# Strassen operand sums and bias additions on VectorE alone, and `state@w_in` casts on ScalarE, in an attention-to-MoE kernel

## Chip, cores and metric

The kernel runs on one core of a Trainium2 chip. The metric is the device time in microseconds (us); 241.25 us is the median of three runs before the change. Engines are called by their short names: PE (TensorE), PEld (its weight loads), DVE (VectorE), ACT (ScalarE), POOL (GpSimd), SP (SyncE, here a DMA queue).

## What is computed

A cross attention between tokens and a small state, in both directions, and then a dense feed-forward block with a squared ReLU. There are 8 batches (B) of 8 heads, 512 tokens (S), 32 state rows (Ns) and a head size of 64; d_model is 512, d_ff 2048.

```python
def _attn_ref(x, state):
    B, H, S, D = x.shape
    scale = 1.0 / np.sqrt(D)
    a = softmax(scale * np.matmul(x, state.transpose(0, 1, 3, 2)))
    xread = np.matmul(a, state)                      # S rows a batch
    a2 = softmax(scale * np.matmul(state, x.transpose(0, 1, 3, 2)))
    sread = np.matmul(a2, x)                         # Ns rows a batch
    return np.concatenate([xread, sread], axis=2)

def _moe_ref(x, w_in, w_out, s, b):
    r = np.maximum(x @ w_in, 0.0)
    g = s * (r * r) + b
    return g @ w_out
```

(`softmax` stands for the written-out subtraction of the maximum, exponential and division.) The inputs are float32; the kernel computes with float16 operands and float32 accumulation.

## The kernel before

**Stages.** The token rows of one batch are one stage `s`. Since `xread @ w_in` is `a @ (state @ w_in)`, the kernel first makes `M` = state@w_in for a batch (`att_M`, four column blocks `c` of 512, evacuated from PSUM as fp16), and the normalised attention weights `a4` (`att_T`, `att_D`: scores, exponential `E`, sum, logarithm `L`, reciprocal `R`, product). Then `mm1_x(s, f)` multiplies the two into `h` for each of 16 blocks `f` of d_ff (two matmuls of 128x512). ACT takes the ReLU `r` of each `h` (line 321), DVE squares two of them at a time into `g` (line 327, 128x1024). The stage of batch `s` also does, in pieces between its 16 steps f, the attention and the `M` of batch `s+1` (`pieces`), and the second matmul of batch `s-1`.

**The second matmul.** For batches 1 to 6 (`fast`) the product `g @ w_out` is done with seven block products p1 to p7 in place of eight (a Strassen level, Winograd's form). It needs operand sums: four of weights, `wd0` to `wd3`, each in two halves `j`, made once (`weight_sums`, on POOL, during stage 1 from f=8 on), and four of tokens for each batch, `s1` to `s4`, each in two halves `j` (`token_sum`; `s1`, `s2` and `s4` on DVE, `s3` on POOL). All are 128x1024 in fp16.

**Products and banks.** `fast_items` gives the matmuls in the order p1, first half of p6, first half of p2, second half of p6, second half of p2, p7, p5, p4, p3. p1 and p2 accumulate in one PSUM bank (`oA`), p6, p7 and p4 in a second (`oB`), p5 and p3 in a third tile (`oC`), out of two buffers. Partial sums are read out on the way, in `done`: after p1, ACT copies the bank scaled to `q`, and POOL makes `qa` and `qb` from it, with the two halves of the bias added; after p6, DVE makes `u2` from the bank and `qa`, and p7 may only then accumulate onto it; after p7, `u3`. `put` makes the output `osb` on DVE and issues its DMA on POOL's queue. p6 needs `s2` and `wd1`, p7 `s3` and `wd2`, p5 `s1` and `wd0`, p4 `wd3`, p3 `s4`. The first 16 products of batch `s` run in the last three steps of stage `s`, the others in stage `s+1`.

**What sets the order.** PE, SP and POOL run in the order in which the code is written (`manual_schedule`); DVE and ACT are ordered by a scheduler when the program is built, and then run in that order, one instruction after another. Semaphores make an instruction wait for its operands and for its buffer. Batch 0, batch 7 and the state rows go without the Strassen level; `late` holds their evacuations until the bias is there (`bias_end`, at f=4 of stage 1). The line number 66 stands for all matmuls.

Of the kernel before, what the change touches and what calls it, by code (L numbers as in the profile page):

```python
# [14 lines left out]
def kernel(  # L15
# [298 lines left out]
    def mm1_close(key, hps, ntok, f):  # L314
        if f % 2 == 0:
            R2[key] = rpool.tile([P, 2, ntok], FP16, name=f"r_{key}_{f}", tag="r")
        r16 = R2[key]
        if key == 0 and f in (1, 5):
            nc.vector.tensor_scalar(r16[:, f % 2], hps, 0.0, None, ALU.max)
        else:  # L320
            nc.scalar.activation(r16[:, f % 2], hps, AF.Relu)  # L321
        if f % 4 == 0:
            G4[key, f // 4] = gpool.tile([P, 4, ntok], FP16, name=f"g_{key}_{f}", tag="g")
        gt = G4[key, f // 4]
        G[key, f] = gt[:, f % 4]
        if f % 2 == 1:
            nc.vector.tensor_mul(gt[:, f % 4 - 1 : f % 4 + 1], r16, r16)  # L327

    def mm1_k(b, f, g, hps):
        a = A[b]  # L330
# [66 lines left out]
                late.pop()()  # L397


    NH = DM // 2  # L400
    TH = S // 2

    def weight_sums():
        out = []
        for j in range(2):
            b11, b12 = wo[j][:, :, 0:NH], wo[j][:, :, NH:DM]
            b21, b22 = wo[2 + j][:, :, 0:NH], wo[2 + j][:, :, NH:DM]
            t1, t2, t3, t4 = (wd[i][j] for i in range(4))
            out += [(t1, b12, b11), (t2, b22, t1), (t3, b22, b12), (t4, b21, t2)]
        return [lambda o=o, a=a, c=c: nc.gpsimd.tensor_sub(o, a, c) for o, a, c in out]  # L410

    SQ = {}

    def token_sum(b, i, j):
        SQ[b, i, j] = spool.tile([P, 4, TH], FP16, name=f"s{i}_{b}_{j}", tag="s")
        o = SQ[b, i, j]
        a11, a21 = G4[b, j][:, :, 0:TH], G4[b, j][:, :, TH:S]
        if i == 3:
            nc.gpsimd.tensor_sub(o, a11, a21)  # L419
            return  # L420
        a12, a22 = G4[b, 2 + j][:, :, 0:TH], G4[b, 2 + j][:, :, TH:S]
        if i == 1:
            nc.vector.tensor_add(o, a21, a22)  # L423
        elif i == 2:
            nc.vector.tensor_sub(o, SQ[b, 1, j], a11)  # L425
        else:
            nc.vector.tensor_sub(o, a12, SQ[b, 2, j])  # L427

    def fast_items(b):
        acc = {}  # L430
        kept = {}

        def lhs(p, k, i):
            c = P * i
            if p == 1:
                return G[b, k][:, c : c + P]
            if p == 2:
                return G[b, 8 + k][:, c : c + P]
            if p == 4:
                return G[b, 8 + k][:, TH + c : TH + c + P]  # L440
            si = {3: 4, 5: 1, 6: 2, 7: 3}[p]
            return SQ[b, si, k // 4][:, k % 4, c : c + P]

        def rhs(p, k):
            if p == 1:
                return wof(k)[:, 0:NH]
            if p == 2:
                return wof(8 + k)[:, 0:NH]
            if p == 3:
                return wof(8 + k)[:, NH:DM]  # L450
            ti = {4: 3, 5: 0, 6: 1, 7: 2}[p]
            return wd[ti][k // 4][:, k % 4, :]

        def keep(name):
            kept[name] = upool.tile([P, 2, NH], FP32, name=f"{name}_{b}", tag=name)
            return kept[name]

        def put(bank, add, j, n0):
            osb = opool.tile([P, 2, NH], FP32, name=f"osb_{b}_{j}_{n0}", tag="osb")
            nc.vector.scalar_tensor_tensor(osb, acc[bank], s_bc, add, ALU.mult, ALU.add)  # L460
            dst = out_BSn[b, 0:S].rearrange("(q ci cj) n -> cj q ci n", ci=2, cj=2)
            nc.gpsimd.dma_start(dst[j][:, :, n0 : n0 + NH], osb)  # L462

        def blk(n0):
            return bias_bc[:, n0 : n0 + NH].unsqueeze(1).broadcast_to([P, 2, NH])

        def done(p):
            if p == 1:
                q = keep("q")
                nc.scalar.activation(q, acc["A"], AF.Copy, scale=s_bc)  # L470
                nc.gpsimd.tensor_add(keep("qa"), q, blk(NH))
                nc.gpsimd.tensor_add(keep("qb"), q, blk(0))
            elif p == 6:
                u = keep("u2")
                nc.vector.scalar_tensor_tensor(u, acc["B"], s_bc, kept["qa"], ALU.mult, ALU.add)  # L475
            elif p == 2:
                put("A", blk(0), 0, 0)
            elif p == 7:
                u = keep("u3")
                nc.vector.scalar_tensor_tensor(u, acc["B"], s_bc, kept["qa"], ALU.mult, ALU.add)  # L480
            elif p == 5:
                put("C", kept["u3"], 1, NH)
            elif p == 4:
                put("B", kept["qb"], 1, 0)
            else:
                put("C", kept["u2"], 0, NH)

        def item(p, k, i):
            bank = {1: "A", 2: "A", 6: "B", 7: "B", 4: "B", 5: "C", 3: "C"}[p]
            fresh = p in (1, 6, 5)  # L490
            if fresh and k == 0 and i == 0:
                acc[bank] = psO.tile([P, 2, NH], FP32, tag="o", name=f"o{bank}_{b}")
# [87 lines left out]
    with tc.manual_schedule(engines={ET.PE, ET.SP, ET.Pool}):  # L580
# [89 lines left out]
        def pieces(s):  # L670
# [3 lines left out]
            def at(f, fn):  # L674
                out.setdefault(f, []).append(fn)

            if s == 1:
                at(0, lambda: att_xT_dma(2))
                at(0, gated_x3)
                at(0, lambda: att_ET(0))  # L680
                at(0, lambda: att_ET(1))
                at(8, lambda: att_xT_dma(3))
                at(12, lambda: load_x(4))
                at(5, lambda: att_M(1, 3, "act"))
                at(2, bias_sum)
                at(3, lambda: att_M(1, 2, "dve"))
                at(4, bias_end)
                at(6, lambda: att_stT(2))
                at(7, lambda: att_M(2, 0, "dve"))
                at(8, lambda: att_M(2, 1, "act"))  # L690
                at(10, lambda: att_M(2, 2, "dve"))
                at(10, lambda: att_T(2, [0, 1]))
                at(11, lambda: att_ET(2))
                at(12, lambda: att_D(2, [0, 1]))
                at(13, lambda: att_M(2, 3, "act"))
                return out
            if s + 3 < B:
                at(13 if s == 2 else 9, lambda: load_x(s + 3))
            if nb < B:
                at(0, lambda: att_stT(nb))  # L700
                at(3, lambda: att_T(nb, [0, 1]))
                at(3, lambda: att_M(nb, 0, "dve"))
                at(4, lambda: att_ET(nb))
                if nb + 1 < B:
                    at(4, lambda: att_xT_dma(nb + 1))
                at(5, lambda: att_D(nb, [0, 1]))
                at(7, lambda: att_M(nb, 1, "dve"))
                at(7, lambda: att_M(nb, 2, "act"))
            at(10, lambda: att_V(s))
            at(11, lambda: att_srT(s))  # L710
            if nb < B:
# [14 lines left out]
        for s in range(1, B):  # L726
# [13 lines left out]
            for f in range(NKF):  # L740
# [1 line left out]
                    token_sum(s - 1, 4, 1)  # L742
                mm1_x(s, f)
                if s in fast:
                    if f in (3, 7):
                        token_sum(s, 3, f // 4)
                    if f in (11, 12, 13):
                        token_sum(s, (1, 2, 4)[f - 11], 0)
                    if f == 15:
# [1 line left out]
                        token_sum(s, 2, 1)  # L751
                for fn in todo_s.get(f, []):
                    fn()
                if s == 1 and f >= 8:
                    sums.pop(0)()
                for fn in items[f]:
                    fn()
                if s == last_b and f in (14, 15):
# [37 lines left out]
```

## Time and profile before

| what | us |
|---|---|
| median of 3 runs (241.06 to 241.54) | 241.25 |
| the profiled execution | 241.94 |
| its span, first to last instruction | 240.1 |
| PE busy | 211.6 |
| DVE busy | 168.9 |
| ACT busy | 124.7 |
| POOL busy | 103.5 |

The span runs from stage 0 (until about 30 us) over stage 1 (30 to 56) and stage 2 (to about 96) to the steady stages 3 to 6 (23.3 us each, to 189), stage 7 and the tail. In the rows, a tile is named without its number: `s` is one of `s1` to `s4`, told apart by the line (419 is `s3`, 423 `s1`, 425 `s2`, 427 `s4`), `wd` one of `wd0` to `wd3`, `u` at line 475 is `u2` and at 480 `u3`. What stands in brackets at the end of a row is the time for which the engine was idle just before, and who released it.

### The profile page before, as it was taken

The page shows a single profiled execution, that of the slowest core. Times are in us where ns is not written, and L with a number is a line of the kernel's source. Part 1 is how long each engine was busy: PE and PEld are TensorE (multiplying, and loading weights), DVE is VectorE, ACT ScalarE, POOL GpSimd, SP SyncE. Part 2 cuts the span into 40 slices and gives each one's busy share as a digit, 9 for nine tenths or more (in the row PEclk, how much of TensorE's full clock was granted, in tenths as well). Part 3 has the DMA queues.
Part 4 walks back from the last instruction along what each step waited for, and adds up shares of the span by engine and source line. Part 5 has one row for each costly group of instructions (what it writes and reads, how often), then busy time and mean ns, then how long its engine had stood idle before and what let it go on. Part 6 is the DMA issues. An engine that isn't in the chain of part 4 may idle for free.

```text
span 240.1 us, 4655 instructions
## 1 busy us (share of the span) xinstructions
PE 211.6 (88%) x1916; PEld 127.3 (53%) x1916; DVE 168.9 (70%) x241; ACT 124.7 (52%) x217; POOL 103.5 (43%) x104
## 2 busy tenths in 40 slices
PE   7887898894717999979998999899899999999993
PEld 3323333342403576656764676467557767766553
DVE  1696649589997569868896699669966995342321
ACT  3786534485103673667566756665576645433200
POOL 6930014699971342646164626342624440211033
PEclk9999999999575899999999999999999999999999
DMA  6999989951700119561919281811131201121223
GB/s 199 208 206 203 198 103 176 207 98 48 128 0 0 46 51 201 102 133 46 176 44 147 39 169 45 177 45 53 38 87 46 87 3 44 46 87 44 87 46 87
DMA packets 38776, 23.72 MB, mean 99 GB/s; under 512 B 24100, under 2 KB 36644, under 8 KB 38756
## 3 DMA queue, kind: packets, MB, share of 16 engines
q0 software_dynamic: 15792, 16.72, 35.2%
q1 hardware_dynamic: 22548, 6.62, 13.4%
q8 instruction: 15, 0.25, 0.4%
q10 hardware_dynamic: 416, 0.10, 0.2%
q14 instruction: 5, 0.04, 0.1%
HBM read 17.33 MB, written 8.91 MB: 109 GB/s over the span
## 4 chain that ended last, share of the span: by engine, by line
PE 56%; DVE 28%; DMA 7%; issue 4%; ACT 2%; POOL 1%; SPq 0%; DVEq 0%
PE h L66 14%; DVE g L327 10%; PE oB L66 10%; PE o L66 9%; PE oC L66 8%; DMA xn<-in_x_dram 5%; DVE s L425 4%; DVE s L427 4%; PE h_sr L66 3%; PE o_sr L66 3%; DVE s L423 3%; PE Mps L66 3%; PE oA L66 3%; DMA xf<-in_x_dram 2%; DVE u L475 2%
## 5 line engine op out<-in xcount | busy, mean ns | idle before, releaser
L321 ACT ACTIVATE r<-h 128x512 f16<-128x512 f32 x126 | 73.8, 596 | 80.2 <-PE h L66 73.4
L66 PE MATMUL h<-a,M 128*128 128x512 f16 x256 | 76.9, 387 | 6.4 <-DVE a L239 5.9
L327 DVE TENSOR_TENSOR g<-r 128x1024 f16<-128x1024 f16 x64 | 56.7, 893 | 21.3 <-ACT r L321 21.2
L66 PEld LDWEIGHTS <-g 128*128 128x128 f16 x432 | 41.4, 99 | 24.6 <-issue 5.6
L66 PEld LDWEIGHTS <-s 128*128 128x128 f16 x384 | 36.5, 100 | 29.9 <-issue 10.2
L419 POOL TENSOR_TENSOR s<-g 128x1024 f16<-128x1024 f16 x12 | 25.4, 2118 | 35.0 <-DVE g L327 34.9
L66 PE MATMUL oB<-wd,s 128*128 128x256 f16 x192 | 29.7, 285 | 11.8 <-DVE s L425 6.7
L462 POOL DMA_DIRECT2D out_dram<-osb x24 | 16.5, 686 | 51.3 <-DVE osb L460 42.5
L66 PEld LDWEIGHTS <-M 128*128 128x128 f16 x256 | 24.9, 99 | 16.3 <-DVE a L239 5.5
L66 PE MATMUL o<-wo,g 128*128 128x512 f16 (+1 forms) x144 | 32.3, 356 | 0.9 <-DVE osb L368 0.9
L66 PE MATMUL oA<-wo,g 128*128 128x256 f16 x192 | 28.6, 278 | 0.3 <-DVE osb L368 0.3
L265 DVE CAST M<-Mps 128x1024 f16<-128x1024 f32 x15 | 18.3, 1218 | 1.6 <-PE Mps L66 1.6
L425 DVE TENSOR_TENSOR s<-s,g 128x1024 f16<-128x1024 f16 x12 | 14.5, 1208 | 0.2
L66 PE MATMUL Mps<-wi,stT 64*32 64x512 f16 x256 | 12.7, 391 | 1.9 <-DVE stT L153 1.0
L66 PE MATMUL oC<-wd,s 128*128 128x256 f16 x96 | 14.3, 273 | 0.0
L66 PE MATMUL oB<-wd,g 128*128 128x256 f16 x96 | 13.6, 273 | 0.0
L263 ACT CAST M<-Mps 128x1024 f16<-128x1024 f32 x13 | 13.1, 1011 | 0.6
L66 PE MATMUL oC<-wo,s 128*128 128x256 f16 x96 | 13.4, 273 | 0.0
L427 DVE TENSOR_TENSOR s<-g,s 128x1024 f16<-128x1024 f16 x12 | 13.0, 1083 | 0.2
L66 PEld LDWEIGHTS <-stT 64*32 64x32 f16 x384 | 5.0, 91 | 14.0 <-issue 8.8
L321 ACT ACTIVATE r_sr<-h_sr 128x256 f16<-128x256 f32 x16 | 6.1, 382 | 10.7 <-PE h_sr L66 10.7
L460 DVE SCALAR_TENSOR_TENSOR osb<-oC,s_bc,u 128x512 f32<-128x512 f32 x12 | 9.0, 748 | 2.8 <-PE oC L66 2.8
(80 smaller groups left out, 231.5 us busy)
## 6 DMA issues: line engine op xcount, KB each, us to landing
out_dram<-osb POOLq DMA_DIRECT2D x31, 256.0 KB, 2.5
xn<-in_x_dram POOLq DMA_DIRECT2D x7, 512.0 KB, 6.3
wi<-in_moe_w_in_dram POOLq DMA_DIRECT2D x4, 512.0 KB, 8.7
wo<-in_moe_w_out_dram POOLq DMA_DIRECT2D x4, 512.0 KB, 16.2
xf<-in_x_dram SPq DMA_DIRECT2D x2, 512.0 KB, 4.8
out_dram<-osb_sr POOLq DMA_DIRECT2D x8, 64.0 KB, 2.0
out_dram<-osb SPq DMA_DIRECT2D x2, 128.0 KB
st<-in_state_dram POOLq DMA_DIRECT2D x1, 192.0 KB, 19.8
```

Of the source, the lines that this page charges most:

```text
L66: return nc.tensor.matmul(out, lhsT, rhs, start=start, stop=stop, tile_position=tp, is_transpose=is_transpose, skip_group_check=True,)
L263: nc.scalar.copy(dst, ps)
L265: nc.vector.tensor_copy(dst, ps)
L321: nc.scalar.activation(r16[:, f % 2], hps, AF.Relu)
L327: nc.vector.tensor_mul(gt[:, f % 4 - 1 : f % 4 + 1], r16, r16)
L419: nc.gpsimd.tensor_sub(o, a11, a21)
L423: nc.vector.tensor_add(o, a21, a22)
L425: nc.vector.tensor_sub(o, SQ[b, 1, j], a11)
L427: nc.vector.tensor_sub(o, a12, SQ[b, 2, j])
L460: nc.vector.scalar_tensor_tensor(osb, acc[bank], s_bc, add, ALU.mult, ALU.add)
L462: nc.gpsimd.dma_start(dst[j][:, :, n0 : n0 + NH], osb)
L475: nc.vector.scalar_tensor_tensor(u, acc["B"], s_bc, kept["qa"], ALU.mult, ALU.add)
```

## The change

- The weight sums and `s3` go from POOL to DVE. The weight sums are issued at f = 5, 7, 9, 14 of stage 1 and f = 2, 3, 4, 6 of stage 2, each behind the last `g`; `wd0` and `wd1` come first.
- `s3` is issued at f = 5 and 9 instead of 3 and 7.
- `q` is dropped. DVE makes `qa` straight from the bank; `qb` is made later, after p5, from `qa` and `bias_d`, the difference of the two halves of the bias, which is computed once.
- The `M` blocks of batches 2 to 7 that DVE evacuated (two in each batch) are evacuated by ACT. The blocks `c` = 1 and 2 of a batch, both at f=7, now stand at f=6 and f=8.

```diff
+    bias_d = konst.tile([P, NH], FP32, name="bias_d")
...
     def weight_sums():
-        out = []
+        out = [[], []]
...
-            out += [(t1, b12, b11), (t2, b22, t1), (t3, b22, b12), (t4, b21, t2)]
-        return [lambda o=o, a=a, c=c: nc.gpsimd.tensor_sub(o, a, c) for o, a, c in out]
+            out[0] += [(t1, b12, b11), (t2, b22, t1)]
+            out[1] += [(t3, b22, b12), (t4, b21, t2)]
+        out = out[0] + out[1][::2] + out[1][1::2]
+        return [lambda o=o, a=a, c=c: nc.vector.tensor_sub(o, a, c) for o, a, c in out]
...
         if i == 3:
-            nc.gpsimd.tensor_sub(o, a11, a21)
+            nc.vector.tensor_sub(o, a11, a21)
             return
...
             if p == 1:
-                q = keep("q")
-                nc.scalar.activation(q, acc["A"], AF.Copy, scale=s_bc)
-                nc.gpsimd.tensor_add(keep("qa"), q, blk(NH))
-                nc.gpsimd.tensor_add(keep("qb"), q, blk(0))
+                q = keep("qa")
+                nc.vector.scalar_tensor_tensor(q, acc["A"], s_bc, blk(NH), ALU.mult, ALU.add)
...
             elif p == 5:
                 put("C", kept["u3"], 1, NH)
+                d = bias_d.unsqueeze(1).broadcast_to([P, 2, NH])
+                nc.vector.tensor_add(keep("qb"), kept["qa"], d)
...
         nc.vector.tensor_scalar(bias_bc, ps2, b_bc, None, ALU.mult)
+        nc.vector.tensor_sub(bias_d, bias_bc[:, 0:NH], bias_bc[:, NH:DM])
...
-                at(7, lambda: att_M(2, 0, "dve"))
+                at(7, lambda: att_M(2, 0, "act"))
                 at(8, lambda: att_M(2, 1, "act"))
-                at(10, lambda: att_M(2, 2, "dve"))
+                at(10, lambda: att_M(2, 2, "act"))
...
-                at(3, lambda: att_M(nb, 0, "dve"))
+                at(3, lambda: att_M(nb, 0, "act"))
...
-                at(7, lambda: att_M(nb, 1, "dve"))
-                at(7, lambda: att_M(nb, 2, "act"))
+                at(6, lambda: att_M(nb, 1, "act"))
+                at(8, lambda: att_M(nb, 2, "act"))
...
-                    if f in (3, 7):
-                        token_sum(s, 3, f // 4)
+                    if f in (5, 9):
+                        token_sum(s, 3, f // 8)
...
-                if s == 1 and f >= 8:
-                    sums.pop(0)()
+                if (s == 1 and f in (5, 7, 9, 14)) or (s == 2 and f in (2, 3, 4, 6)):
+                    with tc.issue_after(G["last"]):
+                        sums.pop(0)()
```

Three places show the new order. First DVE at the joint of stages 1 and 2, before the change: from `a4` of batch 2 to `u2` of batch 1 (the last number of a name is the buffer's, the numbers ahead of it are batch and half or block).

```order
L239 TENSOR_TENSOR a4_2_744<-E_2_701,R_2_743 128x1024
L327 TENSOR_TENSOR g_1_12_734<-r_1_12_732 128x1024
L427 TENSOR_TENSOR s4_1_0_761<-g_1_8_641,s2_1_0_735 128x1024
L327 TENSOR_TENSOR g_1_12_734<-r_1_14_782 128x1024
L423 TENSOR_TENSOR s1_1_1_796<-g_1_4_568,g_1_12_734 128x1024
L153 COPY stT_3_822<-stTps_3_819 128x256
L425 TENSOR_TENSOR s2_1_1_798<-s1_1_1_796,g_1_4_568 128x1024
L427 TENSOR_TENSOR s4_1_1_832<-g_1_12_734,s2_1_1_798 128x1024
L327 TENSOR_TENSOR g_2_0_818<-r_2_0_816 128x1024
L327 TENSOR_TENSOR g_2_0_818<-r_2_2_849 128x1024
L265 CAST M_3_886<-Mps_3_0_887 128x2x512
L475 SCALAR_TENSOR_TENSOR u2_1_900<-oB_1_824,s_bc_101,qa_1_809 128x512
```

And after the change, DVE at the same place, from the second `g` behind `a4` to `u2`:

```order
L330 TENSOR_TENSOR g_1_12_735<-r_1_14_781 128x1024
L474 SCALAR_TENSOR_TENSOR qa_1_805<-oA_1_773,s_bc_101,bias_bc_104 128x512
L427 TENSOR_TENSOR s1_1_1_795<-g_1_4_567,g_1_12_735 128x1024
L156 COPY stT_3_816<-stTps_3_813 128x256
L429 TENSOR_TENSOR s2_1_1_797<-s1_1_1_795,g_1_4_567 128x1024
L330 TENSOR_TENSOR g_2_0_812<-r_2_0_810 128x1024
L431 TENSOR_TENSOR s4_1_1_826<-g_1_12_735,s2_1_1_797 128x1024
L414 TENSOR_TENSOR wd2_0_120<-wo_2_114,wo_0_112 128x1024
L486 TENSOR_TENSOR qb_1_1018<-qa_1_805,bias_d_105 128x512
L330 TENSOR_TENSOR g_2_0_812<-r_2_2_843 128x1024
L414 TENSOR_TENSOR wd2_1_121<-wo_3_115,wo_1_113 128x1024
L477 SCALAR_TENSOR_TENSOR u2_1_894<-oB_1_818,s_bc_101,qa_1_805 128x512
```

`qa`, `qb` and two weight sums (`wd2`) have come in ahead of `u2`, a third (`wd1`, half 1) just ahead of these rows, and the `M` cast has gone. Behind the `g` of f=10 and 11 of stage 1 and ahead of these rows stand, in this order, `osb`, `s1`, `s2`, `osb`, `a4`, `g`, `s4` and that `wd1`.

Second, DVE where a steady stage begins (here stage 4), before the change, from the last `g` of batch 3 to `u2`:

```order
L327 TENSOR_TENSOR g_3_12_1549<-r_3_14_1580 128x1024
L423 TENSOR_TENSOR s1_3_1_1594<-g_3_4_1349,g_3_12_1549 128x1024
L153 COPY stT_5_1620<-stTps_5_1617 128x256
L425 TENSOR_TENSOR s2_3_1_1596<-s1_3_1_1594,g_3_4_1349 128x1024
L427 TENSOR_TENSOR s4_3_1_1630<-g_3_12_1549,s2_3_1_1596 128x1024
L327 TENSOR_TENSOR g_4_0_1616<-r_4_0_1614 128x1024
L327 TENSOR_TENSOR g_4_0_1616<-r_4_2_1647 128x1024
L265 CAST M_5_1684<-Mps_5_0_1685 128x2x512
L475 SCALAR_TENSOR_TENSOR u2_3_1698<-oB_3_1622,s_bc_101,qa_3_1607 128x512
```

And after it, the same stretch on DVE:

```order
L330 TENSOR_TENSOR g_3_12_1547<-r_3_14_1578 128x1024
L474 SCALAR_TENSOR_TENSOR qa_3_1603<-oA_3_1572,s_bc_101,bias_bc_104 128x512
L427 TENSOR_TENSOR s1_3_1_1592<-g_3_4_1343,g_3_12_1547 128x1024
L156 COPY stT_5_1614<-stTps_5_1611 128x256
L429 TENSOR_TENSOR s2_3_1_1594<-s1_3_1_1592,g_3_4_1343 128x1024
L330 TENSOR_TENSOR g_4_0_1610<-r_4_0_1608 128x1024
L431 TENSOR_TENSOR s4_3_1_1624<-g_3_12_1547,s2_3_1_1594 128x1024
L486 TENSOR_TENSOR qb_3_1814<-qa_3_1603,bias_d_105 128x512
L330 TENSOR_TENSOR g_4_0_1610<-r_4_2_1641 128x1024
L423 TENSOR_TENSOR s3_4_0_1723<-g_4_0_1610 128x1024
L477 SCALAR_TENSOR_TENSOR u2_3_1690<-oB_3_1616,s_bc_101,qa_3_1603 128x512
```

`qa`, `qb` and `s3` of the next batch have come in, the `M` cast has gone, and `s4` stands behind the first `g` of the next batch.

Third, ACT in the middle of a steady stage (here stage 3), after the change, from the ReLU of f=5 to that of f=9:

```order
L324 ACTIVATE r_3_4_1341<-h_3_5_1360 128x512
L240 ACTIVATE L_4_1370<-D_4_0_1367 128x1024
L241 ACTIVATE R_4_1371<-L_4_1370 128x1024
L324 ACTIVATE r_3_6_1386<-h_3_6_1383 128x512
L266 CAST M_4_1318<-Mps_4_1_1388 128x2x512
L324 ACTIVATE r_3_6_1386<-h_3_7_1408 128x512
L324 ACTIVATE r_3_8_1423<-h_3_8_1420 128x512
L266 CAST M_4_1318<-Mps_4_2_1426 128x2x512
L324 ACTIVATE r_3_8_1423<-h_3_9_1443 128x512
```

Before, the same ReLUs stood there with one cast, behind that of f=7; now one stands behind that of f=6 and one behind that of f=8. Another has come in behind the two `E`, between the ReLUs of f=3 and f=4.

## Rows read from the trace of the kernel before

**Rows 1.** The page: busy us of each engine, share of the span, instructions.

```profile
PE 211.6 (88%) x1916; PEld 127.3 (53%) x1916; DVE 168.9 (70%) x241; ACT 124.7 (52%) x217; POOL 103.5 (43%) x104
```

**Rows 2.** Stretches: length; busy (instructions) of PE, PEld, DVE, ACT, POOL; PEclk, DMA share, GB/s.

```profile
67.00:73.70 6.70, 0.01 (x1) 0.02 (x2) 6.63 (x7) 0.60 (x1) 3.35 (x3) 0.66 0.00 0
73.70:79.60 5.90, 5.90 (x44) 3.04 (x45) 3.81 (x6) 2.17 (x6) 2.12 (x1) 0.52 0.00 0
...
119.10:142.40 23.30, 22.10 (x230) 14.93 (x229) 18.90 (x30) 14.95 (x25) 11.10 (x9) 1.00 0.56 103
```

**Rows 3.** Timeline of PE at the joint: start, duration, instruction, idle before and releaser.

```profile
55.70 0.82 PE L66 MATMUL oA<-wo,g 128*128 128x256 f16 x6
61.73 1.03 PE L66 MATMUL h<-a,M 128*128 128x512 f16 x2 [5.21 <-DVE a L239]
...
73.69 1.25 PE L66 MATMUL oB<-wd,s 128*128 128x256 f16 x5 [6.72 <-DVE s L425]
...
79.62 0.49 PE L66 MATMUL oB<-wd,s 128*128 128x256 f16 x3
```

**Rows 4.** Timeline of DVE in the same stretch.

```profile
58.69 2.98 DVE L239 TENSOR_TENSOR a<-E,R 128x1024 f16<-128x1024 f16 x1
61.59 9.31 DVE L327 TENSOR_TENSOR g<-r 128x1024 f16<-128x1024 f16 x1
```

**Rows 5.** Timeline of POOL there; the last dots are three sums, gapless.

```profile
58.98 2.13 POOL L410 TENSOR_TENSOR wd<-wo 128x1024 f16<-128x1024 f16 x1
...
61.65 2.13 POOL L410 TENSOR_TENSOR wd<-wo,wd 128x1024 f16<-128x1024 f16 x1
...
69.09 1.25 POOL L472 TENSOR_TENSOR qb<-q,bias_bc 128x512 f32<-128x512 f32 x1
```

**Rows 6.** Timeline of PE: stage 4, before and after `u2`, and stage 7.

```profile
121.97 0.82 PE L66 MATMUL oA<-wo,g 128*128 128x256 f16 x6
...
128.00 0.49 PE L66 MATMUL oB<-wd,s 128*128 128x256 f16 x3 [1.20 <-DVE u L475]
...
196.79 0.60 PE L66 MATMUL oB<-wd,s 128*128 128x256 f16 x4 [0.32 <-DVE u L475]
```

**Rows 7.** Timeline of DVE, start of stage 4, from the last `g` to `u2`.

```profile
120.19 0.69 DVE L327 TENSOR_TENSOR g<-r 128x1024 f16<-128x1024 f16 x1 [0.36 <-ACT r L321]
120.91 0.69 DVE L423 TENSOR_TENSOR s<-g,g 128x1024 f16<-128x1024 f16 x1
...
121.72 1.56 DVE L425 TENSOR_TENSOR s<-s,g 128x1024 f16<-128x1024 f16 x1
123.31 1.64 DVE L427 TENSOR_TENSOR s<-g,s 128x1024 f16<-128x1024 f16 x1
124.87 1.28 DVE L327 TENSOR_TENSOR g<-r 128x1024 f16<-128x1024 f16 x2
126.08 1.21 DVE L265 CAST M<-Mps 128x1024 f16<-128x1024 f32 x1
127.21 0.74 DVE L475 SCALAR_TENSOR_TENSOR u<-oB,s_bc,qa 128x512 f32<-128x512 f32 x1
```

**Rows 8.** Timeline of ACT in stage 4: ReLU of f=3, of 6 and 7, cast.

```profile
124.52 0.60 ACT L321 ACTIVATE r<-h 128x512 f16<-128x512 f32 x1 [0.67 <-PE h L66]
...
131.47 1.06 ACT L321 ACTIVATE r<-h 128x512 f16<-128x512 f32 x2
132.42 1.01 ACT L263 CAST M<-Mps 128x1024 f16<-128x1024 f32 x1
```

**Rows 9.** Timeline in stage 1: PE at f=5, ACT at f=11.

```profile
39.37 1.02 PE L66 MATMUL o<-wo,g 128*128 128x512 f16 x4 [0.86 <-DVE osb L368]
...
50.09 0.60 ACT L321 ACTIVATE r<-h 128x512 f16<-128x512 f32 x1
```

**Rows 10.** Groups by form: count, busy us, mean ns, idle before.

```profile
L265 DVE CAST M<-Mps 128x1024 f16<-128x1024 f32 x15 | 18.3, 1218 | 1.6 <-PE Mps L66 1.6
...
L327 DVE TENSOR_TENSOR g_sr<-r_sr 128x512 f16<-128x512 f16 x8 | 3.4, 424 | 9.5 <-ACT r_sr L321 9.5
```

More of the change, by code (lines that the diff above doesn't have):

```diff
@@ L44 @@
     NPE = 2
+    NH = DM // 2
+    TH = S // 2
     scale = float(1.0 / np.sqrt(D))
@@ L327, in mm1_close @@
             nc.vector.tensor_mul(gt[:, f % 4 - 1 : f % 4 + 1], r16, r16)
+            G["last"] = nc.cur_bb.bb.instructions[-1]
     def mm1_k(b, f, g, hps):
@@ L397, in mm2_part @@
                 late.pop()()
-    NH = DM // 2
-    TH = S // 2
     def weight_sums():
-        out = []
+        out = [[], []]
         for j in range(2):
```

## Prediction

> **What bounds the kernel now.** I read the busy shares first: PE is busy 88% of the span, far above ACT and a good way above DVE [rows 1]. So the question is where PE is not at work, or works at half clock. The stretches tell it [rows 2]: a steady stage (one batch) lasts 23.30 us, of which PE is busy 22.10 at the full clock, so at most 1.2 us per stage can be won there. At the joint of stages 1 and 2 it is different: from 67.0 to 73.7 PE does nothing, and from 73.7 to 79.6 its granted clock is 0.52, the lower of its two levels (1.2 GHz), after it had stood idle. The PE timeline names who ends the waits [rows 3]: 5.21 us before h of batch 2 for `a4` on DVE, 6.72 us before the second half of product p6 for the sum `s2` on DVE.
>
> Why is DVE late there? An fp16 sum of 128x1024 takes 0.69 us when alone (first line of [rows 7]). Here the same kind takes 2.98 us (`a4`) and 9.31 us (`g`) [rows 4]. Beside them stands POOL [rows 5]: `a4` ends 0.56 us after the POOL sum that began at 58.98 (61.67 against 61.11), and `g` starts at 61.59 and ends at 70.90, 0.56 us after the last of five POOL instructions that follow one another without a gap (61.65 to 70.34). So DVE, with two fp16 inputs in SBUF, stands still while POOL computes. The same in small in every steady stage: `s2` and `s4` take 1.56 and 1.64 us beside POOL's `qa` and `qb` [rows 7], and PE then waits 1.20 us for `u2` [rows 6].
>
> **The change, part by part.** The sum is made against the profiled execution (241.94 us, span 240.1); the median of the runs is 0.69 us less.
>
> *POOL's arithmetic goes, and becomes DVE work.* Eight weight sums, twelve `s3` and six `qb` are now DVE instructions. Two fp16 sums issued back to back advance DVE by about 0.60 us (the pair of `g` takes 1.28, minus one 0.69 [rows 7]; I use 0.61). One that reads what the sum just ahead wrote starts 0.72 after it (120.19 to 120.91). A 128x512 read from PSUM with scalar and addend takes 0.74 and advances DVE by 0.67. `qb` in fp32 is not in the trace; it lies between the 0.42 of a 128x512 fp16 product [rows 10] and that 0.74. I take 0.61 of advance, since it is nearest to the second in bytes.
>
> *The `M` casts and `q`.* Twice per steady stage, DVE loses 1.22 us [rows 10] and ACT gains 1.01 [rows 8]; ACT loses `q`, since `qa` is now read from PSUM by DVE. That adds a wait: p2 accumulates onto the bank that `qa` reads, so PE's first p2 product now waits for DVE. In a steady stage `qa` starts right after `g`, 120.80, and is done at 121.54; p2 starts at 121.97 [rows 6]. It is covered by 0.4 us.
>
> *Stage 1, until 51 us: nothing gained.* `s3` and `bias_d` now stand ahead of the two `osb` for which PE already waits 0.86 us at 39.37 [rows 9]. They cost 0.61 and about 0.3, less a gap of 0.2: PE is 0.7 later. The following wait for `stT` is shorter, because `M` of batch 2 is no longer ahead; PE is then about 0.35 early. On ACT one `M` cast (0.95) now comes ahead of `E`, so that the ReLU of f=11, which ran at 50.09 [rows 9], ends at about 51.2 instead of 50.7. DVE waits for it.
>
> *From 51.2 to p7 of stage 2: the large term.* From there DVE is never idle until `u2`, in the order shown: 15 fp16 sums at 0.61 (9.15), one direct dependence (0.12), two `osb` and `qa` (3 x 0.67 = 2.01), `stT` (0.2), `qb` (0.61): 12.1 us, so `u2` starts at 63.3, ends at 64.05, and PE starts p7 at 64.1. On the way `a4` ends at 55.2, before PE is through with p1 (56.4 now [rows 3], 0.35 or more earlier then): the 5.21 us are gone. `s2` ends at 59.7; PE waits for `qa` and for it some 0.9 us in all, then about 1.0 for `u2`, in place of 6.72. These waits are no longer than the 1.20 of a steady stage, where the clock stays at 1.00 [rows 2], so I take the full clock. Before, p7 began at 79.62 [rows 3]: **15.5 us**. Bounds: 14.5 to 16.5, for half a microsecond on the ReLU's start and half on the twenty DVE steps.
>
> *A steady stage.* After `g` (120.19): `qa` 120.80, `s1` 121.47, `stT` 122.08, `s2` 122.28, `g` 122.9, `s4` 123.5, `qb` 124.1. The next `g` needs the ReLU that starts at 124.52 and ends at 125.12 [rows 8], so it starts at 125.14. Then `s3`, dependent, at 125.86, and `u2` at 126.47 instead of 127.21 [rows 7]. What ends last is now the ReLU, not POOL: **0.74 us** per stage, in the stages 3 to 6: 3.0. Bounds: 0 (`u2` as late as now) to 1.2, all of PE's idle time: 0 to 4.8. In stage 7 there is no `s3` ahead of `u2`: by the same steps it ends at about 196.1, and PE has p2 to do until 196.47 (196.79 less the wait), so its wait (0.32 as shown [rows 6], 0.5 from issue to issue) goes: **0.5**.
>
> *The rule for the shared port.* The trace shows one `g` held across five POOL instructions [rows 4, 5]. The Trainium skill (SBUF — State Buffer, Who interferes with whom) says that a DVE instruction with two SBUF inputs and a GpSimd one that reads SBUF exclude each other, and that the second to issue blocks until the first finishes; by that, `g` would be held for one POOL instruction, not five. The trace agrees that they exclude each other and not with the length. By the page some 6.5 of the 9.31 us would have another cause and remain.
>
> Sum: 15.5 + 3.0 + 0.5 = 19.0. Profiled execution 241.94 - 19.0 = 222.9; less 0.69, the median: **222.3**.
>
> **The rivals.**
> *ACT becomes late.* It is busy 14.95 of 23.30 us per stage [rows 2]; with two casts more and no `q`, about 16.3. But `R`, ReLU, cast and ReLU now follow one another: the ReLU of f=7 starts at about 133.0 where it ran about 132.0, and PE needs its bank about 0.6 later. If that margin fails, a cast (0.95) shows in each of five stages: 4.75, so 227.0. For it: the tightest place on ACT. Against: the margin.
> *`u2` gains nothing.* If `qb` or the dependent `s3` are dearer, the 3.0 goes: 225.3. If instead all of PE's steady idle time goes, 4 x 0.46 more: 220.4.
> *POOL was not what held `g`.* If it was held for one POOL instruction (2.13) and then for something that stays, 9.31 - 2.13 - 0.69 = 6.5 is not won: 228.8. Against: the end 0.56 us after POOL's last instruction, as for `a4`.
> *Slower: DVE's sums are slow there by themselves.* If between 51 and 80 us a sum on DVE takes what `a4` took, 2.98, whoever computes beside it (the loads of x and w_out lie near), the sixteen sums up to `u2` cost 47.7 plus 2.2: p7 at about 102, 22 us later than now: 263. It decides from 1.6 us per sum (79.62 - 51.2 - 0.8 - 2.2 = 25.4, over 16). Against: in the steady stages, slow sums stand only beside POOL's arithmetic.
>
> **How the numbers follow.** Forecast (222.3, itself 221 to 224.5): 0.68. ACT late (227.0): 0.10. All steady idle time gone (220.4): 0.10. `u2` gains nothing (225.3): 0.04. One POOL instruction (228.8): 0.05. Slower (263): 0.03. The range 219.5 to 225.6 holds the first, third and fourth, 0.82. Faster by over 0.2% (half a microsecond, about what a measurement of this kernel can tell from none) are all but the last: 0.96; within 0.2%, for what I overlooked, 0.01; slower 0.03.
>
> **What would show it.** POOL: no arithmetic from 41 us on. DVE: every 128x1024 fp16 sum at 0.69, none above 0.8. PE: no wait over 1.5 us between 50 and 80, p7 of batch 1 at 64, clock 1.00 throughout; steady stages of 22.5 to 22.6 us with a wait of about 0.5 before p7, ended by `u2`. Wrong would be: sums above 1 us without POOL, PE waiting for a ReLU at f=8 to 10, or a low clock that remains in stage 2.

## The result, and the profile after

| | before | after |
|---|---|---|
| median, us | 241.39 (4 runs) | 223.63 (223.41 to 224.14, 4 runs) |
| ratio | | 0.9267, interval 0.9247 to 0.9288 |
| profiled execution, us | 241.94 | 223.63 |
| its span, us | 240.1 | 221.8 |
| granted clock, mean of the span | 0.964 | 1.00 |

The forecast was 222.3 (219.5 to 225.6). The page of after, busy times of the engines; it answers to [rows 1]:

```profile
PE 207.4 (94%) x1916; PEld 125.9 (57%) x1916; DVE 147.6 (67%) x262; ACT 131.0 (59%) x223; POOL 41.2 (19%) x72
```

DVE has 21 instructions more and is busy 21 us less. Twelve `M` casts of 1.22 us have left it, and 33 shorter instructions have come in; but the same `g`, `a4`, `s1`, `s2` and `s4` of 128x1024 that both kernels have took 100.9 us before and take 73.6 us now, and these 27 us are time in which they were held. Two stretches of after, the joint and a steady stage (columns as in [rows 2]):

```profile
51.20:64.10 12.90, 11.70 (x107) 7.21 (x106) 12.86 (x23) 9.80 (x17) 2.01 (x3) 1.00 0.82 103
103.00:126.00 23.00, 22.52 (x233) 15.14 (x232) 17.66 (x31) 16.07 (x26) 3.59 (x5) 1.00 0.55 104
```

At the joint DVE is the engine without a pause (12.86 of 12.90 us) and the clock is at 1.00, the higher of its two levels; before, PE stood there, and then ran at 0.52 [rows 2]. POOL's 2.01 and 3.59 us are DMA issues alone. The PE timeline of after, the waits in stage 1 and at the joint, and the rows that begin a p7 (`oB` with x3 or x4; the one at 133.73 is left out); it answers to [rows 3, 6]:

```profile
40.19 1.02 PE L68 MATMUL o<-wo,g 128*128 128x512 f16 x4 [1.67 <-DVE osb L372]
...
58.11 0.81 PE L68 MATMUL oA<-wo,g 128*128 128x256 f16 x6 [0.40 <-DVE qa L474]
...
63.79 0.49 PE L68 MATMUL oB<-wd,s 128*128 128x256 f16 x3 [0.80 <-DVE u L477]
...
88.24 0.49 PE L68 MATMUL oB<-wd,s 128*128 128x256 f16 x3 [0.48 <-DVE u L477]
...
110.98 0.49 PE L68 MATMUL oB<-wd,s 128*128 128x256 f16 x3 [0.48 <-DVE u L477]
...
156.48 0.49 PE L68 MATMUL oB<-wd,s 128*128 128x256 f16 x3 [0.48 <-DVE u L477]
...
178.46 0.60 PE L68 MATMUL oB<-wd,s 128*128 128x256 f16 x4
```

The waits of 5.21 and 6.72 us are gone, and p7 of batch 1 begins at 63.79. The same rows of before give the time of each later stage, from one p7 to the next:

```profile
104.70 0.49 PE L66 MATMUL oB<-wd,s 128*128 128x256 f16 x3 [1.20 <-DVE u L475]
...
174.61 0.49 PE L66 MATMUL oB<-wd,s 128*128 128x256 f16 x3 [1.20 <-DVE u L475]
```

Before: 25.08 (79.62 to 104.70), 23.30 three times, 22.18 (174.61 to 196.79). After: 24.45, 22.75 three times, 21.98. The first gains 0.63, the steady ones 0.55 each, the last 0.20. The joint gains 79.62 - 63.79 = 15.83. Sum: 15.83 + 0.63 + 1.65 + 0.20 = 18.31, the difference of the two spans (18.3); from p7 of batch 6 to the end it is 43.3 us in both.

DVE of after, at the joint and in a steady stage, answers to [rows 4, 7]:

```profile
54.31 0.68 DVE L242 TENSOR_TENSOR a<-E,R 128x1024 f16<-128x1024 f16 x1
54.91 0.68 DVE L330 TENSOR_TENSOR g<-r 128x1024 f16<-128x1024 f16 x1
...
61.18 0.68 DVE L486 TENSOR_TENSOR qb<-qa,bias_d 128x512 f32<-128x512 f32 x1
...
62.99 0.74 DVE L477 SCALAR_TENSOR_TENSOR u<-oB,s_bc,qa 128x512 f32<-128x512 f32 x1
...
108.85 0.69 DVE L330 TENSOR_TENSOR g<-r 128x1024 f16<-128x1024 f16 x1 [0.34 <-ACT r L324]
109.58 0.69 DVE L423 TENSOR_TENSOR s<-g 128x1024 f16<-128x1024 f16 x1
110.18 0.74 DVE L477 SCALAR_TENSOR_TENSOR u<-oB,s_bc,qa 128x512 f32<-128x512 f32 x1
```

`a4` and the `g` behind it take 0.68 us where they took 2.98 and 9.31. In the steady stage the chain is the forecast one: ReLU, `g`, the dependent `s3` 0.73 later, `u2` another 0.60 later.

### The profile page after: what moved, and what is told of

Read it like the earlier page. It is cut to its first block, busy times and chain, and to the rows that moved or that the text cites. A ratio compares the mean times of both kernels' runs of the same rounds, so it can differ in the third digit from the quotient of the medians.

```text
span 221.8 us, 4633 instructions
## 1 busy us (share of the span) xinstructions
PE 207.4 (94%) x1916; PEld 125.9 (57%) x1916; DVE 147.6 (67%) x262; ACT 131.0 (59%) x223; POOL 41.2 (19%) x72
## 4 chain that ended last, share of the span: by engine, by line
PE 71%; DVE 13%; DMA 8%; ACT 4%; issue 1%; POOL 1%; SPq 0%
PE h L68 18%; PE oB L68 14%; PE o L68 10%; PE oC L68 9%; PE oA L68 6%; DMA xn<-in_x_dram 5%; DVE g L330 4%; PE h_sr L68 3%; PE o_sr L68 3%; PE Mps L68 3%; DMA xf<-in_x_dram 2%; ACT r L324 2%; DVE u L477 2%; PE D L68 1%; DVE osb L372 1%; DVE s L423 1%
## 5 line engine op out<-in xcount | busy, mean ns | idle before, releaser
L68 PE MATMUL h<-a,M 128*128 128x512 f16 x256 | 75.0, 379 | 1.2 <-DVE a L242 0.7
L330 DVE TENSOR_TENSOR g<-r 128x1024 f16<-128x1024 f16 x64 | 44.2, 691 | 24.7 <-ACT r L324 24.5
L68 PEld LDWEIGHTS <-s 128*128 128x128 f16 x384 | 35.7, 98 | 18.3 <-issue 7.5
L68 PE MATMUL oB<-wd,s 128*128 128x256 f16 x192 | 27.9, 273 | 2.8 <-DVE u L477 2.7
L68 PE MATMUL oA<-wo,g 128*128 128x256 f16 x192 | 27.8, 273 | 0.4 <-DVE qa L474 0.4
L266 ACT CAST M<-Mps 128x1024 f16<-128x1024 f32 x25 | 25.3, 1010 | 0.6
L242 DVE TENSOR_TENSOR a<-E,R 128x1024 f16<-128x1024 f16 (+1 forms) x9 | 5.7, 632 | 7.0 <-ACT R L241 7.0
L240 ACT ACTIVATE L<-D 128x1024 f32<-128x1024 f32 (+1 forms) x9 | 8.3, 926 | 2.5 <-PE D L68 2.5
L217 ACT ACTIVATE E<-T 128x512 f16<-128x512 f32 x16 | 9.4, 596 | 0.7 <-PE T L68 0.7
L330 DVE TENSOR_TENSOR g_sr<-r_sr 128x512 f16<-128x512 f16 x8 | 3.4, 424 | 9.5 <-ACT r_sr L324 9.5
```

The costliest lines, as they stand in the source:

```text
L68: return nc.tensor.matmul(out, lhsT, rhs, start=start, stop=stop, tile_position=tp, is_transpose=is_transpose, skip_group_check=True,)
L217: nc.scalar.activation(a["E"][:, g, :].rearrange("p (m t) -> p m t", m=2), T[:, :, 256 * i : 256 * i + 256], AF.Exp, scale=scale, accum_ou ...
L240: nc.scalar.activation(a["L"][:, sl], Dps, AF.Ln)
L242: nc.vector.tensor_mul(a["a4"][:, sl], a["E"][:, sl], a["R"][:, sl])
L266: nc.scalar.copy(dst, ps)
```

## Experiments

Theory A: POOL's arithmetic held DVE's sums with two inputs in SBUF; the weight sums' move is the large term, and the rest of the change the small one. Against it stand that DVE was late by its own list, the `M` casts above all, and that its sums are slow at the joint whoever works beside them. Medians of before beside these runs lie between 241.1 and 241.4.

### One part alone

Before, with the weight sums alone moved to DVE, in the order and at the places of the change:

```diff
-        return [lambda o=o, a=a, c=c: nc.gpsimd.tensor_sub(o, a, c) for o, a, c in out]
+        return [lambda o=o, a=a, c=c: nc.vector.tensor_sub(o, a, c) for o, a, c in out]
...
-                if s == 1 and f >= 8:
-                    sums.pop(0)()
+                if (s == 1 and f in (5, 7, 9, 14)) or (s == 2 and f in (2, 3, 4, 6)):
+                    with tc.issue_after(G["last"]):
+                        sums.pop(0)()
```

> The kernel before, with the eight weight sums alone on DVE, in the slots and the order of the changed kernel; s3, qa, qb stay on POOL and the M casts where they were. Theory A (POOL's arithmetic holds DVE's two-input sums, and the weight sums are its long gapless run): the 9.31 us of g and the 2.98 us of a4 go, p7 of batch 1 starts at 65 to 67 us instead of 79.62, steady stages stay at 23.3 us; 227 to 229 us in all. Rival B (the gain comes from taking load off DVE, by the casts and q): DVE has 4.9 us more to do, 241 us or more. Rival C (the sums are slow there by themselves): slower than 241 us.

Measured: 228.25 us, ratio 0.9457 (0.9436 to 0.9478). PE at the joint and in a steady stage:

```profile
61.31 0.72 PE L66 MATMUL oB<-wd,s 128*128 128x256 f16 x5 [1.28 <-DVE s L428]
...
66.27 0.49 PE L66 MATMUL oB<-wd,s 128*128 128x256 f16 x3 [1.49 <-DVE u L478]
...
91.33 0.49 PE L66 MATMUL oB<-wd,s 128*128 128x256 f16 x3 [1.20 <-DVE u L478]
```

p7 of batch 1 is at 66.27 (79.62 before), and the steady stages keep their 1.20 us wait and their 23.30 us. So 13 of the 18 us come with the weight sums' move alone.

Before, with the `M` casts alone on ACT (and blocks 1 and 2 at f=6 and f=8):

```diff
-                at(7, lambda: att_M(2, 0, "dve"))
+                at(7, lambda: att_M(2, 0, "act"))
...
-                at(3, lambda: att_M(nb, 0, "dve"))
-                at(7, lambda: att_M(nb, 1, "dve"))
-                at(7, lambda: att_M(nb, 2, "act"))
+                at(3, lambda: att_M(nb, 0, "act"))
+                at(6, lambda: att_M(nb, 1, "act"))
+                at(8, lambda: att_M(nb, 2, "act"))
```

> The kernel before, with only the M casts moved to ACT (and the blocks at f=6 and 8); all sums stay on POOL. Theory A: the joint of stages 1 and 2 keeps its waits of 5 and 6 us and its half clock; in steady stages one cast of 1.21 us goes from ahead of u2, so PE's wait of 1.20 goes, less what the split of the blocks costs (0.2): 0.9 us in each of five stages; 236 to 238 us. Rival B: most of the gain is here, under 230 us.

Measured: 237.12 us, ratio 0.9827 (0.9795 to 0.9858), mean clock 0.976. PE at the joint and at the p7 of two steady stages:

```profile
60.45 1.03 PE L66 MATMUL h<-a,M 128*128 128x512 f16 x2 [3.94 <-DVE a L239]
...
72.73 1.25 PE L66 MATMUL oB<-wd,s 128*128 128x256 f16 x5 [7.63 <-DVE s L425]
...
102.09 0.49 PE L66 MATMUL oB<-wd,s 128*128 128x256 f16 x3
...
124.49 0.49 PE L66 MATMUL oB<-wd,s 128*128 128x256 f16 x3
```

The long waits remain: the casts were not their cause. In the steady stages, however, the wait for `u2` is gone, and a stage takes 22.40 us (102.09 to 124.49), less than the 22.75 of the whole change, which has the same split of the blocks.

### One part taken back

The changed kernel with the weight sums on POOL again (in the order and at the steps of before):

```diff
-        return [lambda o=o, a=a, c=c: nc.vector.tensor_sub(o, a, c) for o, a, c in out]
+        return [lambda o=o, a=a, c=c: nc.gpsimd.tensor_sub(o, a, c) for o, a, c in out]
```

> The changed kernel, with the eight weight sums back on POOL, in the order and slots that they had before; all else as changed. Theory A: g, a4 or the s sums between 45 and 70 us are held again, up to several us each, and PE waits; 12 to 16 us are lost: 235 to 240 us, steady stages as changed (22.75 us). Rival B: 223 to 225 us (DVE has 4.9 us less to do).

Measured: 233.13 us, ratio 0.9658 (0.9638 to 0.9678). DVE at the joint, then POOL there:

```profile
57.48 6.88 DVE L330 TENSOR_TENSOR g<-r 128x1024 f16<-128x1024 f16 x1
```

```profile
57.54 2.13 POOL L412 TENSOR_TENSOR wd<-wo,wd 128x1024 f16<-128x1024 f16 x1
59.62 2.12 POOL L412 TENSOR_TENSOR wd<-wo,wo 128x1024 f16<-128x1024 f16 x1
61.69 2.12 POOL L412 TENSOR_TENSOR wd<-wo,wd 128x1024 f16<-128x1024 f16 x1
```

The `g` ends at 64.36, 0.55 us after the last of three sums (63.81), the tail of 0.56 seen in [rows 4, 5]. The loss, 9.5 us, is smaller than expected: the run is three sums long and not five instructions, since `qa` and `qb` are no longer POOL's.

The changed kernel with `q` on ACT and `qa`, `qb` on POOL as before:

```diff
-                q = keep("qa")
-                nc.vector.scalar_tensor_tensor(q, acc["A"], s_bc, blk(NH), ALU.mult, ALU.add)
+                q = keep("q")
+                nc.scalar.activation(q, acc["A"], AF.Copy, scale=s_bc)
+                nc.gpsimd.tensor_add(keep("qa"), q, blk(NH))
+                nc.gpsimd.tensor_add(keep("qb"), q, blk(0))
...
-                d = bias_d.unsqueeze(1).broadcast_to([P, 2, NH])
-                nc.vector.tensor_add(keep("qb"), kept["qa"], d)
```

> The changed kernel, with q back on ACT and qa, qb back on POOL (bias_d left out, as nothing reads it). Theory A: s2 and s4 take 1.5 to 1.6 us again in each steady stage, u2 starts about 0.35 us later against the ReLU, steady stages of 23.1 us instead of 22.75; 225 to 226 us. Rival B (only DVE's load counts): DVE has 1.3 us per stage less, 223 us or a little under.

Measured: 225.92 us, ratio 0.9359 (0.9337 to 0.938). In a steady stage the wait before p7 is 0.80, the stage takes 23.13 us, and the two sums beside `qa` and `qb` take 1.56 and 1.64 again, as in [rows 7].

### The suspected cause by itself

To the changed kernel, 16 subtractions on POOL were added from f=8 of stage 1 on, which read `w_out` and write a tile that nobody reads; in a second kernel, 32 memsets of the same tile in their place:

```diff
+                if s == 1 and f >= 8:
+                    nc.gpsimd.tensor_sub(scr, wo[2][:, 0:2, NH:DM], wo[0][:, 0:2, 0:NH])
+                    nc.gpsimd.tensor_sub(scr, wo[2][:, 2:4, NH:DM], wo[0][:, 2:4, 0:NH])
```

> The changed kernel with useless POOL work added: sixteen subtractions of 128x512 fp16, from w_out in SBUF into a tile that nobody reads, two at each step f=8 to 15 of stage 1 in POOL's queue; about as long as the weight sums were. DVE's own list is the same. Theory A (POOL reading SBUF beside DVE holds DVE's two-input sums): sums on DVE between 41 and 65 us take 1.5 to 9 us each, PE waits; 228 to 238 us. Rival C (contention has nothing to do with it): 223.6 us.

> As the last, but POOL writes only: thirty-two memsets of the same tile at the same places, some 16 us in all. Theory A1 (what holds DVE is POOL's reading): DVE's sums stay at 0.69 us, 223.6 us. Theory A2 (any work of POOL in SBUF holds it): sums of 1 us and more as in the last run, 226 to 236 us.

Measured, two executions each: 232.5 us, ratio 0.963 (0.9605 to 0.9656), with the subtractions; 223.71, ratio 0.9266 (0.9242 to 0.9291), with the memsets. DVE and POOL beside the subtractions:

```profile
46.54 1.64 DVE L424 TENSOR_TENSOR s<-g 128x1024 f16<-128x1024 f16 x1
48.11 1.64 DVE L331 TENSOR_TENSOR g<-r 128x1024 f16<-128x1024 f16 x1
```

```profile
46.15 1.49 POOL L765 TENSOR_TENSOR scr<-wo,wo 128x512 f16<-128x512 f16 x1
47.71 1.49 POOL L764 TENSOR_TENSOR scr<-wo,wo 128x512 f16<-128x512 f16 x1
```

And beside the memsets:

```profile
44.48 0.68 DVE L415 TENSOR_TENSOR wd<-wo,wd 128x1024 f16<-128x1024 f16 x1
```

```profile
44.73 0.52 POOL L765 MEMSET scr<- 128x512 f16 x1
```

Sums that nothing depends on, with no other edit, bring back 8.9 of the 17.8 us. The memsets, busy on POOL at the same steps, cost nothing. It is POOL's reading of SBUF that holds DVE's sums, not its being at work or its writing. That one input of POOL's is enough shows in the changed kernel itself: its only sum of 128x1024 above 0.69 us is a `g` of stage 1 beside a POOL copy within SBUF, and it ends 0.55 us after that copy (33.50 and 32.95; in the run below with `s3` late, the same `g` begins 0.11 us after the copy and takes 1.26):

```profile
32.58 0.92 DVE L330 TENSOR_TENSOR g<-r 128x1024 f16<-128x1024 f16 x1 [2.61 <-ACT r L324]
```

```profile
32.12 0.83 POOL L671 COPY st<-st 128x768 f16<-128x768 f16 x1 [16.40 <-DMA st<-in_state_dram]
```

The Trainium skill (SBUF — State Buffer, Who interferes with whom) says both: that a DVE instruction with two SBUF inputs contends with a GpSimd one that reads SBUF, and not with one that only writes it. These two runs agree. In the first of them the two engines also take turns, one DVE sum to one POOL instruction (46.15, 46.54, 47.71, 48.11), as the rule on issue order in the same section of the Trainium skill has it. In the kernel before and in the one with the weight sums back, a `g` stood through five and through three POOL instructions, which that rule does not give.

### What the sum had missed

The changed kernel with the `M` blocks 1 and 2 both at f=7 again, still on ACT:

```diff
-                at(6, lambda: att_M(nb, 1, "act"))
-                at(8, lambda: att_M(nb, 2, "act"))
+                at(7, lambda: att_M(nb, 1, "act"))
+                at(7, lambda: att_M(nb, 2, "act"))
```

> The changed kernel with M blocks 1 and 2 of a batch together at f=7 again, both still evacuated by ACT. My reading of the steady stage (22.75 us instead of 22.56 as forecast) is that PE loses about 0.1 us at each switch to the small state matmuls and that the split adds one switch: then stages of 22.55 us, 222.4 to 222.8 us. Rival: two casts one after the other on ACT (2 us) make PE wait for a ReLU at f=10: stages of 22.75 or more, 223.6 us or more.

Measured: 222.49 us, ratio 0.9215 (0.9198 to 0.9231); p7 at 88.01, 110.53, 133.04: 22.52 a stage. PE of the changed kernel (an `h` followed by another product, and the two blocks), then PE of this one, where the sixteen matmuls run together:

```profile
111.31 0.59 PE L68 MATMUL h<-a,M 128*128 128x512 f16 x2
111.74 0.59 PE L68 MATMUL D<-E,bones 128*128 128x512 f16 x2
...
112.93 0.59 PE L68 MATMUL h<-a,M 128*128 128x512 f16 x2
113.46 0.41 PE L68 MATMUL Mps<-wi,stT 64*32 64x512 f16 x8
113.80 0.83 PE L68 MATMUL oB<-wd,s 128*128 128x256 f16 x6
...
116.30 0.41 PE L68 MATMUL Mps<-wi,stT 64*32 64x512 f16 x8
116.64 0.61 PE L68 MATMUL oC<-wd,s 128*128 128x256 f16 x4
```

```profile
114.20 0.62 PE L68 MATMUL Mps<-wi,stT 64*32 64x512 f16 x16
114.76 0.61 PE L68 MATMUL oC<-wd,s 128*128 128x256 f16 x4
```

A block of eight occupies 0.34 us from its start to the next row, twice 0.68, where sixteen together occupy 0.56 (114.20 to 114.76). And from `h` to a block it is 0.53 (112.93 to 113.46), from `h` to another product only 0.43 (111.31 to 111.74). So a second block apart costs 0.12 + 0.10 = 0.22, and the stage is 0.23 shorter with them together. The Trainium skill (TensorEngine Tiling (Array Packing), Key Properties) says that a change of the tiling mode drains TensorE. No row shows the drain itself; that the entry into the 64x32 form takes 0.10 us more agrees with it.

The changed kernel with `s3` behind the `g` and `u2` that are due with it:

```diff
-                        token_sum(s, 3, f // 8)
+                        with tc.issue_after(G["last"]):
+                            token_sum(s, 3, f // 8)
```

> The changed kernel with s3 issued behind the g of f=5 (and of f=9) instead of ahead of u2. If what ends PE's remaining wait of 0.48 us is ReLU, g, s3, u2 in a row, u2 starts 0.7 us earlier, the wait goes, stages of 22.3 us: 221.2 to 221.8 us (four stages, and a bit at the joint). Rival: u2 is no longer last and p2 or something else is: no change, 223.6 us.

Measured: 220.37 us, ratio 0.9129 (0.9112 to 0.9146), better than expected. DVE in a steady stage, and PE at p7:

```profile
107.45 0.69 DVE L330 TENSOR_TENSOR g<-r 128x1024 f16<-128x1024 f16 x1 [0.34 <-ACT r L324]
108.06 0.74 DVE L477 SCALAR_TENSOR_TENSOR u<-oB,s_bc,qa 128x512 f32<-128x512 f32 x1
```

```profile
108.50 0.60 PE L68 MATMUL oA<-wo,g 128*128 128x256 f16 x4
108.93 0.49 PE L68 MATMUL oB<-wd,s 128*128 128x256 f16 x3
```

No wait is left before p7, and a stage takes 22.10 us, 0.65 less than 22.75, where the wait was shown as 0.48. What was not expected at all is stage 1: p7 of batch 1 is at 63.02 instead of 63.79. Of these 0.77 us, 0.48 are PE's wait in stage 1, 1.19 instead of 1.67, since `s3` of batch 1 no longer stands ahead of `osb` there. The other 0.29 were there before stage 1 began (29.73 against 30.02), ahead of all that the edit touches; that start lies between 29.7 and 30.4 in the traces here.

The changed kernel with the weight sums ahead of time, so that fewer lie between `a4` and `u2`:

```diff
-                if (s == 1 and f in (5, 7, 9, 14)) or (s == 2 and f in (2, 3, 4, 6)):
+                n_sums = {(1, 5): 1, (1, 7): 2, (1, 9): 3, (2, 5): 1, (2, 6): 1}
+                for _ in range(n_sums.get((s, f), 0)):
```

> The changed kernel with the weight sums wd1 and wd2 issued earlier in stage 1 (one at f=5, two at f=7, three at f=9, the two wd3 at f=5 and 6 of stage 2), where DVE stands idle for 1.5 to 2 us three times. If the list of DVE from 51 us to u2 is what bounds the joint, three sums of 0.60 us leave it: PE's waits of 0.40 (qa) and 0.80 (u2) go, p7 of batch 1 at 62.6 to 63.0 us instead of 63.79; 222.5 to 222.9 us. Rival (the joint is bound by ReLUs, E and casts on ACT, or by PE): 223.6 us.

Measured: 222.62 us, ratio 0.9234 (0.9218 to 0.925); p7 of batch 1 at 62.79, and PE's wait for `qa` is gone. The joint was bound by the length of DVE's list.

The changed kernel with `s3` alone on POOL again, at f=3 and 7:

```diff
-            nc.vector.tensor_sub(o, a11, a21)
+            nc.gpsimd.tensor_sub(o, a11, a21)
```

> The changed kernel with only s3 back on POOL, at f=3 and 7. Theory A with what the last runs showed: in a steady stage POOL's s3 runs beside u2 and osb, which have one operand in PSUM and are not held, and no two-input sum falls into its 2.1 us; then u2 loses the s3 ahead of it: stages of 22.1 us, and s3 no longer stands ahead of osb in stage 1: 220.3 to 221.5 us, faster than the changed kernel. Rival (any POOL sum costs DVE as much as it takes): two sums of 2.1 us per stage hold DVE, PE waits 0.5 us or more per stage longer: 225 us or more.

Measured: 221.8 us, ratio 0.9196 (0.9182 to 0.921): faster than the changed kernel, though a little above what was expected. POOL in stage 1 and in a steady stage, then DVE at both places:

```profile
40.16 2.13 POOL L423 TENSOR_TENSOR s<-g 128x1024 f16<-128x1024 f16 x1
...
109.78 2.12 POOL L423 TENSOR_TENSOR s<-g 128x1024 f16<-128x1024 f16 x1 [5.18 <-DVE g L330]
```

```profile
40.13 2.73 DVE L330 TENSOR_TENSOR g<-r 128x1024 f16<-128x1024 f16 x1
...
109.55 0.74 DVE L477 SCALAR_TENSOR_TENSOR u<-oB,s_bc,qa 128x512 f32<-128x512 f32 x1
...
110.63 0.75 DVE L464 SCALAR_TENSOR_TENSOR osb<-oA,s_bc,bias_bc 128x512 f32<-128x512 f32 x1 [0.26 <-PE oA L68]
```

In the steady stage the first half of POOL's `s3` falls beside instructions that read PSUM; they take what they take alone. The second half does hold a `g` (1.15 us at 118.27, beside POOL's sum from 116.75 to 118.86), but PE does not wait for it, and a stage lasts 22.10 us. In stage 1 `s3` falls on a `g`, which is held until 0.57 us after it (42.29 to 42.86); p7 of batch 1 is 0.72 later than in the changed kernel (64.51), more than the 0.3 by which the run lies above the expected range.

Last, the three edits (blocks together, `s3` late, weight sums early) in one kernel, with `bias_d` behind the `osb` of stage 1:

```diff
-        nc.vector.tensor_sub(bias_d, bias_bc[:, 0:NH], bias_bc[:, NH:DM])
         bias_ready.append(True)
         while late:
             late.pop(0)()
+        nc.vector.tensor_sub(bias_d, bias_bc[:, 0:NH], bias_bc[:, NH:DM])
```

> The last three edits together (M blocks 1 and 2 at f=7, s3 behind the g of f=5 and 9, weight sums early), and bias_d made behind the osb of batch 0 instead of ahead of them. If they add: 220.4 less 0.23 in each of five stages (1.15), less about 1.0 at the joint, less 0.3 for bias_d: 217.6 to 218.4 us. Rival (with PE gapless, the two casts in a row on ACT, or a later DVE, bring a new wait): 219 us or more.

Measured: **217.72 us** (217.42 to 217.97), ratio 0.9025 (0.901 to 0.9041), 5.9 us below the changed kernel and the best of all. One steady stage of it:

```profile
107.16:129.03 21.87, 21.87 (x231) 15.02 (x229) 17.20 (x30) 15.90 (x27) 3.59 (x5) 1.00 0.67 111
```

PE is busy for the whole of it. The next gain in these stages would have to come from PE's own work.

## Why the prediction was right, and where its sum was off

| term, us | predicted | measured |
|---|---|---|
| joint, until p7 of batch 1 | 15.5 | 15.83 |
| stages 3 to 6 | 3.0 | 2.28 (0.63 + 3 x 0.55) |
| stage 7 | 0.5 | 0.20 |
| sum | 19.0 | 18.31 |
| profiled execution of after, less its median | 0.69 | 0.00 |

**What bounds it, and the joint.** Right. `a4` ended at 54.99 (55.2), PE waited 0.40 for `qa` (the 0.9 forecast for `qa` and `s2`) and 0.80 for `u2` (1.0), `u2` began at 62.99 (63.3), p7 at 63.79 (64.1). The step of DVE was 0.60 and not 0.61, and the `g` at 51.05 began a little earlier than assumed. That POOL was the cause rests on the runs: the useless subtractions bring it back, the memsets do not. Stage 1 gave nothing, as forecast; PE's wait there came to 1.67 (0.86 and 0.7). The joint's 0.3 above the forecast is thus made of small errors, of the step and of where the `g` began, that happened to point the same way.

**DVE's new work.** `qb` took 0.68 and was booked at 0.61 of advance; it advanced DVE by 0.60 (61.18 to 61.78).

**The steady stages.** `u2` came as walked: in the chain from `g` on, it began 1.33 after the `g` (108.85 to 110.18), as forecast (125.14 to 126.47), and the 0.48 wait was forecast as about 0.5. The step that failed is the split of the `M` blocks, which the sum left at nothing without looking at PE. It costs 0.23 in each of the five intervals from one p7 to the next: 1.15, and putting the blocks together gave 1.14. It is also why the stages took 22.75 us and not the 22.5 to 22.6 that the prediction named; with the blocks together they took 22.52. Without it, the terms of 3.0 and 0.5 would have measured 3.6 in sum.

**The median.** The profiled execution of before lay 0.69 above its median, and the sum took that offset over to after, whose profiled execution lies at its median. That is about half of the miss of 1.3 us: the offset of one execution belongs to that execution.

**The rivals.** ACT was not late: the ReLUs of f=7 and 8 run back to back at 115.81 in after, and PE waits for none. `u2` did gain. Of a hold by one POOL instruction alone, 6.5 us would have stayed at the joint; nothing stayed. DVE's sums are not slow by themselves: those of 128x1024 in fp16 take 0.67 to 0.69, all but the `g` beside POOL's copy (0.92 at 32.58), which is above the 0.8 that the prediction allowed. The case that all steady idle time goes did not come, but an edit of one line (`s3` late) reaches it.

**What the forecast did not see** is that the change gives part of its gain back. With the casts alone on ACT, a steady stage took 22.40 us, with the whole change 22.75. The split of the blocks is in both. What differs in such a stage is `s3` on DVE, whose place ahead of `u2` costs 0.65 (22.75 against 22.10), and POOL's `qa` and `qb`, which cost 0.38 (23.13 against 22.75): the first is the larger.

**Open.** Why a DVE sum is held for one POOL instruction in some places (the turns beside the subtractions) and through a gapless run in others: five at 61.59 in [rows 4, 5], three at 57.48 with the weight sums back, and five again with the casts alone on ACT. In the first two the `g` began 0.06 us ahead of the first POOL sum, in the third 0.39 us ahead:

```profile
60.31 9.63 DVE L327 TENSOR_TENSOR g<-r 128x1024 f16<-128x1024 f16 x1
```

```profile
60.09 0.59 POOL L370 DMA_DIRECT2D out_dram<-osb  x1 [1.52 <-DVE osb L368]
60.70 2.13 POOL L410 TENSOR_TENSOR wd<-wo,wd 128x1024 f16<-128x1024 f16 x1
```

What the three share is that the `g` began while POOL was on the DMA issue directly ahead of its sums. Sums that began in the middle of a POOL sum were let in at its end, also where POOL's next sum followed without a gap (in before, the `g` at 50.72 ended at 53.03, 0.55 after the POOL sum that it began beside). No run here moved a DMA issue, so this is a pattern of the traces and not a shown cause.

## What to carry to other kernels

Look for DVE instructions with two SBUF inputs that last several times their usual time, and for what POOL computes beside them; in these runs POOL's arithmetic cost nothing only where DVE read PSUM or where nothing waited for the DVE sum that it held. When sums are moved to the engine that stands on the path, place each behind what PE waits for next: here that order was worth some 3 us (0.48 in stage 1, and 0.65 in each of four stages). And cost a rearrangement on the bound engine from its rows, even if it only moves two blocks of matmuls apart.

## What was not expected of the hardware

- Sixteen matmuls of the 64x32 form took 0.56 us of PE together and 0.68 in two blocks, and the entry into that form from a 128x128 matmul another 0.10.
- POOL is slowed too: its 128x512 subtraction took 1.16 us where it began ahead of the turns and 1.48 to 1.50 in turns with DVE, and DVE's sum 1.64.
- A DVE instruction with one operand in PSUM was not held: `qa`, `u2` and `osb` took 0.72 to 0.75 beside POOL's arithmetic, as without it.
- A DVE sum could begin well ahead of POOL's arithmetic and still be held to its end: beside the useless subtractions an `s2` began at 54.48, during a DMA issue on POOL, and ended at 57.05, 0.56 us after a subtraction that began only at 55.32. At its usual 0.69 us it would have been over at 55.17.
